# Attention scores over one head's 64 rows, the two heads alternating between the halves of TensorE

## The chip, the cores and the metric

The kernel runs on one core of a Trainium2 chip. The core's engines work side by side: TensorE (PE) multiplies matrices into PSUM, VectorE (DVE), ScalarE (ACT) and GpSimd (POOL) do the elementwise work, and SyncE (SP) issues most DMA. What counts is the device time of one execution in microseconds (us), as the median of several runs.

## The reference

What is computed is one attention block followed by two feed-forward blocks, over 4 batches, 8 heads, 576 tokens and 64 elements per head (512 per token):

```python
scores = (1 / sqrt(64)) * q @ k.T                 # per batch and head, 576 x 576
scores = where(pos[:, None] // 64 >= pos[None, :] // 64, scores, -1e9)
attn = softmax(scores) @ v                        # heads side by side give x, 576 x 512
x = x + relu(layernorm(x) * g @ w1_1) @ w2_1      # first feed-forward, 512 -> 2048 -> 512
u = x + real(fft(fft(x, tokens), features))       # mixing
out = u + relu(layernorm(u) @ w1_2) @ w2_2        # second feed-forward
```

## The kernel before, in words

Heads are taken two at a time: 4 batches of 4 pairs. The 64 elements of one head lie on partitions 0 to 63 and those of the other on 64 to 127, so q and k of a pair fill 128 partitions. A product of one head alone then has to keep the other head out, and the kernel does that with zeros: one operand is held with zeros in the other head's half, and the product runs over all 128 partitions.

The attention has two parts. The early queries (`e_...`, the first 256 tokens of each batch) are handled first, in f32: `e_raw` loads q of a pair and, into halves 1 and 2 of a tile `rz` whose other halves were set to zero once, k of the one and of the other head. There are three such tiles (`RAWE`), used in turn. `e_s` multiplies them into a score tile `st` of two PSUM banks, one per head, for a query block of 128 (128 keys) and a second one (256 keys), and `mask` adds a large negative number to the last 64 keys of the rows that may not see them (a product of the constant tiles `late` and `never`).

The late queries (`a_...`) come as f16 high and low parts. `a_split` writes q into `qz`, again with zeros in the other head's half, and k into `k`. `a_s` handles one of three query blocks j of a pair: for j = 2 (384 keys) and j = 3 (512 keys) three passes per head (high by high, low by high, high by low), all three of one head and then all three of the other, and two masks; for j = 4 (576 keys) 64 queries of each head share a product over all 128 partitions. `a_exp` takes the maximum on VectorE and the exponential on ScalarE, `a_norm_p` splits the result, a DMA transposes it, `a_pv` multiplies by the values.

All of it is recorded by one planner, `merge`, which takes the next step of several streams (early attention, late attention, feed-forward blocks, weight decoding) by due times made of fixed costs; a tile framework then orders single instructions by priority and by its own model of when each can start. Each engine executes its instructions in the order so fixed. Between two attention steps on TensorE stand one or two feed-forward blocks (`gemm1` at L626, `gemm2` at L651 and L678). The second half of the program (mixing and the second feed-forward) holds no attention.

Lines of before: `e_raw` loads at L882 and L885, `mask` at L917, `e_s` at L949, `a_s` at L1164, value products at L897, zeroing of `rz` at L1589.

Of the kernel before, what the change touches and what calls it, by code (L numbers as in the profile page):

```python
# [8 lines left out]
F32 = mybir.dt.float32  # L9
# [11 lines left out]
NPAIR = H // 2  # L21
# [8 lines left out]
RAWE = 3  # L30
# [68 lines left out]
def fused_kernel(ctx: ExitStack, tc: tile.TileContext, io: dict):  # L99
    nc = tc.nc  # L100
# [33 lines left out]
    late = cpool.tile([128, 3, 128], BF16, name="late")  # L134
    never = cpool.tile([128, 64], BF16, name="never")
# [668 lines left out]
    A = {}  # L804
    ap_ = {}

    def prio(f, n=None):
        def g(*a):
            if (n or AP) <= 0:
                return f(*a)  # L810
            with tc.high_priority(n or AP):
                return f(*a)
        return g
# [6 lines left out]
    def a_tile(shape, dt, tag, name):  # L820
        return ap_["p"].tile(shape, dt, tag=tag, bufs=ap_["b"][tag], name=name)
# [56 lines left out]

    def e_raw(b, p):

        r = A["rz"][(NPAIR * b + p) % RAWE]
        nc.sync.dma_start(out=r[:, 0], in_=io["qt"][b, p][:, S:S + 256])  # L882
        for h in range(2):
            hs = slice(64 * h, 64 * h + 64)
            nc.sync.dma_start(out=r[hs, 1 + h], in_=io["kt"][b, p][hs, 0:256])  # L885
        A["raw", b, p] = r

    def v_tiles(n, name):
# [23 lines left out]
        )  # L912
        A["ev", b] = (vh, vl, s)

    def mask(out, k):

        nc.tensor.matmul(out=out, lhsT=late[:, k, :], rhs=never, start=False, stop=True)  # L917

    def p_split(e, P, n):

# [22 lines left out]
    @(lambda f: prio(f, ESP))  # L943
    def e_s(b, p):
        r = A.pop(("raw", b, p))
        st = pss.tile([128, 2, 512], F32, tag="s", name="st")
        for t, (o, w) in enumerate(EO):
            for h in range(2):
                nc.tensor.matmul(  # L949
                    out=st[:, h, o:o + w], lhsT=r[:, 0, 128 * t:128 * t + 128], rhs=r[:, 1 + h, 0:w],  # L950
                    start=True, stop=False,
                )
            for h in range(2):
                mask(st[:, h, o + w - 64:o + w], 0)
        A["st", b, p] = st

    def e_exp(b, p):
# [85 lines left out]
    def e_items(b):  # L1043
        def head():
            e_raw(b, 0)
            e_load(b)

        def front(p):
            if p + 1 < NPAIR and b not in ET:
                e_raw(b, p + 1)  # L1050
            e_s(b, p)
            e_exp(b, p)
            e_norm_p(b, p)
# [5 lines left out]
        def two():  # L1059
            for p in range(2):  # L1060
                e_s(b, p)
                e_exp(b, p)
            in_order(lambda: (busy(NBUSY, A["busy"][:, 0:384]), e_norm_p(b, 0)) if b == 0 else e_norm_p(b, 0))

        if b in ET:
            return [
                (0.0, lambda: [e_raw(b, p) for p in range(3 if b == 0 else 2)], (), None),
                (4.0, lambda: (two(), e_load(b)), (), None),
                (2.0, lambda: (e_raw(b, 2) if b else None, e_norm_p(b, 1)), (), None),
                (3.0, lambda: (e_raw(b, 3), front(2), back(0)), (), None),  # L1070
                (3.0, lambda: (front(3), back(1)), (), None),
                (1.0, lambda: back(2), (), None),
                (1.0, lambda: back(3), (), ("X1", ("E", b))),
            ]
# [77 lines left out]
    @prio  # L1152
    def a_s(u, j):
        qz, k = A["op", u][0]
        st = pss.tile([128, 2, 512], F32, tag="s", name="st")
        sf = st.rearrange("p a f -> p (a f)")
        w = 128 * j + (128 if j < 4 else 64)
        for o in range(0, w, 512):
            n = min(w - o, 512)
            for h in range(2 if j < 4 else 1):  # L1160
                q = 384 * h + 128 * (j - 2)
                passes = ((0, 0), (1, 0), (0, 1))
                for i, (a, c) in enumerate(passes):
                    nc.tensor.matmul(  # L1164
                        out=st[:, h, 0:n] if j < 4 else sf[:, o:o + n],
                        lhsT=qz[:, a, q:q + 128], rhs=k[:, c, o:o + n],
                        start=(i == 0), stop=(j == 4 and i == 2),
                    )
        if j < 4:
            for h in range(2):  # L1170
                mask(st[:, h, w - 64:w], j - 1)
        A["st", u, j] = st[:, :, 0:w] if j < 4 else sf[:, 0:w].rearrange("p (o k) -> p o k", o=1)

    def a_exp(u, j):
# [85 lines left out]
    def attention_items(order):  # L1260
# [14 lines left out]
        for t, (u, j) in enumerate(units):  # L1275
            at(t, RK[0], a_s, u, j)
            at(t + lag[1], RK[1], a_exp, u, j)
            at(t + lag[2], RK[2], a_norm_p, u, j)
            at(t + lag[3], RK[3], a_pv, u, j)
            at(t + lag[4], RK[4], a_evac, u, j)  # L1280
            if j == 4 and u[1] == NPAIR - 1:
                at(t + lag[5], RK[5], a_x, u[0])
                gives[t + lag[5]] = ("X1", ("F", u[0]))
# [263 lines left out]
    if True:  # L1547
# [5 lines left out]
        nc.vector.memset(late, 0.0)  # L1553
        nc.vector.memset(never, float(-2.0 ** 120))
        for k, a, z in ((0, 0, 64), (1, 0, 32), (1, 33, 64), (1, 127, 128), (2, 64, 128)):
            nc.vector.memset(late[0:1, k, a:z], 1.0)
        F3 = ("F", 3)
        EF = [(h, b) for h in "EF" for b in range(B)]
        order1 = [x if x == "L" else (x[0], int(x[1])) for x in ORDER1.split()]
# [23 lines left out]
        A["busy"] = g_tile([128, 512], "busy")  # L1583
        busy(8, A["busy"][:, 0:384])
        A["unit"] = a_tile([128, 128], F32, "unit", "unit")
        A["rz"] = [a_tile([128, 3, 256], F32, "rz", f"rz{i}") for i in range(RAWE)]
        for z in A["rz"]:
            for h in range(2):
                nc.gpsimd.memset(z[64 - 64 * h:128 - 64 * h, 1 + h], 0.0)  # L1589
        nc.gpsimd.dma_start(out=A["unit"], in_=io["c_unit"])  # L1590
        w_signs(ap_["p"], WN[0], NZ[0])
        AE = [e_items(b) for b in range(B)]
# [209 lines left out]
```

## Time and profile before

| | us |
|---|---|
| median of 3 runs | 990.58 (988.44 to 992.95) |
| profiled execution | 996.84 |
| its span, first to last instruction | 995.0 |
| TensorE busy in the span | 937.5 (94%) |
| VectorE busy | 707.0 (71%) |
| ScalarE busy | 541.6 (54%) |
| mean granted clock of TensorE | 0.984 of full speed |

Busy time is what the records of an engine cover. A matmul's record reaches from its start to a modelled end, and the next one starts before that end; so from start to start is what a product costs in a row of products, and the record's own length is longer. Idle time of an engine that is not the bound costs nothing.

### The profile page before, as it was taken

How to read it: one execution, taken by the hardware profiler on the slowest of the kernel's cores; microseconds unless marked ns; L12 is line 12 of the kernel's file. 1: busy time of each engine (PE TensorE's matmuls, PEld its weight loads, DVE VectorE, ACT ScalarE, POOL GpSimd, SP SyncE). 2: the span in 40 equal slices, each digit the busy share in tenths (PEclk: the TensorE clock that was granted, in tenths of full speed). 3: DMA queues.
4: the chain of work that ended last, by engine and by line, in shares of the span. 5: the costliest groups of instructions: out<-in, count | busy, mean ns of one | idle time of the engine just before them, and what ended most of it. 6: DMA issues, size and time to landing. Idle time of an engine off the chain costs nothing.

```text
span 995.0 us, 19877 instructions
## 1 busy us (share of the span) xinstructions
PE 937.5 (94%) x7854; PEld 708.1 (71%) x7854; DVE 707.0 (71%) x1754; ACT 541.6 (54%) x964; POOL 78.4 (8%) x190
## 2 busy tenths in 40 slices
PE   8897899999898999998899799999999999999998
PEld 7795754665674764857485566858588888888887
DVE  3778898787777776556487878569476775765754
ACT  5778757777676776427466644325153352342431
POOL 2000010002011020040022111100000000000000
PEclk9898999999999999999999989999999999999999
DMA  8756546679567674587318666001110101101100
GB/s 254 226 180 204 151 98 141 139 130 180 108 149 142 130 141 90 97 192 276 106 47 237 216 189 212 16 12 64 43 23 23 33 22 33 22 23 43 22 23 22
DMA packets 159453, 110.97 MB, mean 112 GB/s; under 512 B 134397, under 2 KB 141574, under 8 KB 157312
## 3 DMA queue, kind: packets, MB, share of 16 engines
q1 hardware_dynamic: 154896, 104.87, 40.6%
q0 software_dynamic: 2352, 4.32, 1.9%
q8 instruction: 61, 1.00, 0.4%
q10 hardware_dynamic: 2112, 0.52, 0.2%
q14 instruction: 32, 0.26, 0.1%
HBM read 64.19 MB, written 11.01 MB: 76 GB/s over the span
## 4 chain that ended last, share of the span: by engine, by line
PE 42%; DVE 6%; DMA 5%; ACT 3%; issue 1%; POOL 0%; SPq 0%; ACTq 0%; POOLq 0%
PE g L697 15%; PE s L747 13%; PE g L626 5%; PE g L678 4%; PE g L651 3%; DMA wr<-in_w 3%; ACT junk L238 1%; DVE wq L338 1%; DVE ws L217 1%; DMA xnT1('F', 3)_7111<-xs 1%; DMA xnT2('F', 0)_8367<-xs 1%; ACT sign L216 1%; PE ya L1452 1%; DVE hT L636 1%; PE pq L1486 0%
## 5 line engine op out<-in xcount | busy, mean ns | idle before, releaser
L626 PEld LDWEIGHTS <-wq 128*128 128x128 f16 x2112 | 205.3, 99 | 43.9 <-issue 11.6
L651 PE MATMUL g<-wq,hT 128*128 128x512 f16 x768 | 182.4, 384 | 2.8 <-ACT hT L635 2.3
L697 PEld LDWEIGHTS <-wq 128*128 128x128 f16 x1344 | 131.5, 98 | 15.4
L651 PEld LDWEIGHTS <-hT 128*128 128x128 f16 x768 | 74.4, 99 | 89.6 <-issue 4.3
L747 PEld LDWEIGHTS <-hs 128*128 128x128 f16 x1176 | 115.1, 98 | 13.3
L714 ACT ACTIVATE hr<-g,tk 128x256 f32<-128x256 f32 x112 | 47.1, 472 | 141.0 <-PE g L697 141.0
L897 PE MATMUL pv<-vh,PT 128*128 128x65 f16 (+1 forms) x704 | 93.5, 200 | 12.7 <-DMA PT<-P 5.7
L722 DVE TENSOR_TENSOR hr<-hr 128x128 f32<-128x128 f32 x224 | 65.5, 292 | 48.3 <-ACT hr L714 40.3
L897 PEld LDWEIGHTS <-PT 128*128 128x128 f16 x1056 | 73.4, 98 | 20.6 <-issue 8.6
L1186 ACT ACTIVATE e<-st,aq,acf 128x384 f32<-128x384 f32 (+2 forms) x80 | 56.8, 742 | 48.2 <-DVE aq L1181 33.6
L922 DVE SCALAR_TENSOR_TENSOR P<-e,P 128x768 f16<-128x768 f32 (+2 forms) x56 | 54.6, 975 | 37.6 <-ACT P L921 37.5
L747 PE MATMUL s<-tT,hs 128*128 128x256 f16 x672 | 75.6, 273 | 0.0
L636 DVE SCALAR_TENSOR_TENSOR hT<-g,hT 128x512 f16<-128x512 f32 x88 | 59.8, 683 | 21.8 <-ACT hT L635 21.8
L635 ACT ACTIVATE hT<-g 128x512 f16<-128x512 f32 x88 | 51.4, 587 | 30.7 <-PE g L626 30.3
L678 PE MATMUL g<-wq,hT 128*128 128x512 f16 x288 | 64.4, 379 | 0.0
L1164 PE MATMUL st<-k,qz 128*128 128x512 f16 (+2 forms) x288 | 57.3, 330 | 6.9 <-ACT e L1186 6.3
L729 DVE TENSOR_TENSOR hs<-hr,hs 128x896 f16<-128x896 f32 x56 | 60.7, 1084 | 0.5
L216 ACT ACTIVATE sign<-wr 128x512 f16<-128x512 bf16 (+1 forms) x48 | 46.3, 968 | 23.0 <-DMA wr<-in_w 19.6
L897 PE MATMUL pv<-vl,PT 128*128 128x64 f16 (+1 forms) x352 | 58.0, 199 | 0.0
L747 PE MATMUL s<-tB,hs 128*128 128x256 f16 x504 | 57.3, 273 | 0.0
L217 DVE SCALAR_TENSOR_TENSOR ws<-wr,sign 128x512 int32<-128x512 int32 (+1 forms) x48 | 41.3, 865 | 19.7 <-ACT sign L216 17.9
L728 ACT ACTIVATE hs<-hr 128x896 f16<-128x896 f32 x56 | 53.1, 947 | 1.6 <-DVE hr L722 1.6
(434 smaller groups left out, 1607.7 us busy)
## 6 DMA issues: line engine op xcount, KB each, us to landing
wr<-in_w SPq DMA_DIRECT2D x16, 1023.5 KB, 5.6
wr<-in_w SPq DMA_DIRECT2D x32, 511.8 KB, 5.2
rawv<-in_vt SPq DMA_DIRECT2D x16, 320.0 KB, 3.5
rawqk<-in_kt SPq DMA_DIRECT2D x16, 288.0 KB, 2.9
d<-ws SPq DMA_DIRECT2D x4, 1024.0 KB, 5.1
ws<-d SPq DMA_DIRECT2D x4, 1024.0 KB, 5.8
wt<-d SPq DMA_DIRECT2D x4, 1024.0 KB, 4.8
rawqk<-in_qt SPq DMA_DIRECT2D x32, 80.0 KB, 2.9
```

The lines of the kernel that those rows point to most:

```text
L216: nc.scalar.activation(out=z[:, :, :, 1], in_=r.bitcast(BF16)[:, :, :, 2], func=AF.Copy)
L626: nc.tensor.matmul(out=ps[:, i, :], lhsT=w1(ffn, k, wh, m), rhs=xt[:, xh, k, :], start=(n == 0), stop=(n == 3 * KT - 1),)
L636: nc.vector.scalar_tensor_tensor(out=h[:, :, 1, :], in0=ps, scalar=0.0, in1=h[:, :, 0, :], op0=ALU.max, op1=ALU.subtract,)
L651: nc.tensor.matmul(out=ps, lhsT=h[f // 4][:, f % 4, hh, t * 128:(t + 1) * 128], rhs=w2(ffn, f, wh), start=(f == 0 and hh == 0 and wh == 0) ...
L678: nc.tensor.matmul(out=g2["b"][t], lhsT=h[f // 4][:, f % 4, hh, t * 128:(t + 1) * 128], rhs=w2(ffn, f, wh), start=(f == 0 and hh == 0 and ...
L697: nc.tensor.matmul(out=ps[:, q, :], lhsT=w1(2, k, wh, i + 8 * q), rhs=xt[:, xh, k, :], start=(n == 0), stop=(n == 3 * KT - 1),)
L722: done = nc.vector.tensor_tensor(out=r[:, o], in0=r[:, a], in1=r[:, b], op=op)
L729: nc.vector.tensor_tensor(out=h[:, 1], in0=r[:, 1:8], in1=h[:, 0], op=ALU.subtract)
L747: nc.tensor.matmul(out=ps, lhsT=h[:, hh, hb], rhs=T[nm][:, wh, i], start=(i == 0 and hh == 0 and wh == 0), stop=(i == 7 and hh == 1),)
L897: nc.tensor.matmul(out=out[..., 0:w], lhsT=l, rhs=v[..., 0:w], start=(n == 0), stop=(n == len(mm) - 1))
L1164: nc.tensor.matmul(out=st[:, h, 0:n] if j < 4 else sf[:, o:o + n], lhsT=qz[:, a, q:q + 128], rhs=k[:, c, o:o + n], start=(i == 0), stop=(j ...
L1186: nc.scalar.activation(out=e[:, h], in_=st[:, h], func=AF.Exp, scale=cf, bias=nb[:, h:h + 1],)
```

## The change

Three things change. `e_raw` loads all of k of a pair at once into a tile of two parts, a new one from the pool for each pair, and the zero halves and their memsets are gone. `e_s`, `a_s` for j = 2 and 3, and `mask` take their operands from 64 partitions, the lower for the first head and the upper for the second. And `a_s` has the loop over the passes outside that over the heads, so that the heads, and with them the halves of the array and the two banks, alternate from product to product. `late` gets its ones in row 64 too, so that the upper half's mask finds them.

```diff
 def e_raw(b, p):
-        r = A["rz"][(NPAIR * b + p) % RAWE]
+        r = a_tile([128, 2, 256], F32, "rz", f"rz{b}{p}")
         nc.sync.dma_start(out=r[:, 0], in_=io["qt"][b, p][:, S:S + 256])
-        for h in range(2):
-            hs = slice(64 * h, 64 * h + 64)
-            nc.sync.dma_start(out=r[hs, 1 + h], in_=io["kt"][b, p][hs, 0:256])
+        nc.sync.dma_start(out=r[:, 1], in_=io["kt"][b, p][:, 0:256])
...
-    def mask(out, k):
-
-        nc.tensor.matmul(out=out, lhsT=late[:, k, :], rhs=never, start=False, stop=True)
+    HALF = (slice(0, 64), slice(64, 128))
+
+    def mask(out, k, h):
+
+        nc.tensor.matmul(
+            out=out, lhsT=late[HALF[h], k, :], rhs=never[HALF[h]], start=False, stop=True
+        )
...
-                    out=st[:, h, o:o + w], lhsT=r[:, 0, 128 * t:128 * t + 128], rhs=r[:, 1 + h, 0:w],
-                    start=True, stop=False,
+                    out=st[:, h, o:o + w], lhsT=r[HALF[h], 0, 128 * t:128 * t + 128],
+                    rhs=r[HALF[h], 1, 0:w], start=True, stop=False,
                 )
             for h in range(2):
-                mask(st[:, h, o + w - 64:o + w], 0)
+                mask(st[:, h, o + w - 64:o + w], 0, h)
...
-            for h in range(2 if j < 4 else 1):
-                q = 384 * h + 128 * (j - 2)
-                passes = ((0, 0), (1, 0), (0, 1))
-                for i, (a, c) in enumerate(passes):
+            for i, (a, c) in enumerate(((0, 0), (1, 0), (0, 1))):
+                for h in range(2 if j < 4 else 1):
+                    q = 384 * h + 128 * (j - 2)
+                    r = HALF[h] if j < 4 else slice(0, 128)
                     nc.tensor.matmul(
                         out=st[:, h, 0:n] if j < 4 else sf[:, o:o + n],
-                        lhsT=qz[:, a, q:q + 128], rhs=k[:, c, o:o + n],
+                        lhsT=qz[r, a, q:q + 128], rhs=k[r, c, o:o + n],
...
-            nc.vector.memset(late[0:1, k, a:z], 1.0)
+            for r in (0, 64):
+                nc.vector.memset(late[r:r + 1, k, a:z], 1.0)
...
-        A["rz"] = [a_tile([128, 3, 256], F32, "rz", f"rz{i}") for i in range(RAWE)]
-        for z in A["rz"]:
-            for h in range(2):
-                nc.gpsimd.memset(z[64 - 64 * h:128 - 64 * h, 1 + h], 0.0)
```

First, where the loads stand at the program's start on SyncE's queue: `rz` are the tiles of early q and k, `wr` the first feed-forward's raw weights. Before:

```order
2 L882 DMA rz_113<-in_qt 128x256
3 L885 DMA rz_113<-in_kt 64x256 x2
4 L882 DMA rz_114<-in_qt 128x256
5 L885 DMA rz_114<-in_kt 64x256 x2
6 L882 DMA rz_115<-in_qt 128x256
7 L885 DMA rz_115<-in_kt 64x256 x2
8 L201 DMA wr_188<-in_w_1 128x2x2047
```

In this place two loads of k became one, and nothing else moved:

```order
2 L882 DMA rz_121<-in_qt 128x256
3 L883 DMA rz_121<-in_kt 128x256
4 L882 DMA rz_124<-in_qt 128x256
5 L883 DMA rz_124<-in_kt 128x256
6 L882 DMA rz_127<-in_qt 128x256
7 L883 DMA rz_127<-in_kt 128x256
8 L201 DMA wr_184<-in_w_1 128x2x2047
```

Second, TensorE in the early part, a pair of the last batch: `st<-rz` are its score products (L949, now L951), `st<-never,late` the masks, `g<-wq,hT` feed-forward. Before:

```order
1228 L949 MATMUL st<-rz_113 128x128
1229 L678 LDWEIGHTS hT
1230 L678 MATMUL g_1587<-wq_1550,hT 128x512
...
1239 L949 MATMUL st<-rz_113 128x128
1240 L678 LDWEIGHTS hT
1241 L678 MATMUL g_1587<-wq_1550,hT 128x512
1242 L917 LDWEIGHTS late
1243 L917 MATMUL st<-never,late 128x64
```

After the change, the same pair, and ahead of it one of the pairs that still alternate with feed-forward products (`g<-xnT1,wq`, L626), as 5 of the 16 pairs do, here and in before:

```order
812 L951 MATMUL st<-rz_1098 128x128
813 L626 LDWEIGHTS wq_459
814 L626 MATMUL g_1148<-xnT1('E', 1)_848,wq_459 128x256
815 L951 MATMUL st<-rz_1098 128x128
...
1234 L951 MATMUL st<-rz_1484 128x128 x2
1235 L917 LDWEIGHTS late
1236 L917 MATMUL st<-never,late 128x64
```

So single pairs close up, and others stay apart. In the late part the sequence of `a_s`, value and feed-forward blocks on TensorE is the same in both programs; each `a_s` call for j = 2 and 3 stands as one piece of six products and two masks.

## Rows read from the trace of the kernel before

**Rows 1.** The page's busy line, and TensorE's busy and clock slices.
```profile
PE 937.5 (94%) x7854; PEld 708.1 (71%) x7854; DVE 707.0 (71%) x1754; ACT 541.6 (54%) x964; POOL 78.4 (8%) x190
...
PE   8897899999898999998899799999999999999998
...
PEclk9898999999999999999999989999999999999999
```
**Rows 2.** Windows: busy us of each engine in four stages; columns stand first.
```profile
core 0: us, PE busy (x) PEld busy (x) DVE busy (x) ACT busy (x) POOL busy (x), PEclk, DMA share, GB/s
0.00:150.00 150.00, 131.31 (x1073) 104.70 (x1074) 112.32 (x301) 105.74 (x172) 13.91 (x37) 0.95 0.62 185
150.00:425.00 275.00, 255.96 (x2401) 172.03 (x2400) 208.68 (x527) 192.67 (x349) 27.41 (x73) 0.99 0.64 131
425.00:575.00 150.00, 136.32 (x921) 90.70 (x919) 104.94 (x284) 87.28 (x177) 28.31 (x58) 0.98 0.60 185
575.00:995.00 420.00, 413.89 (x3465) 340.70 (x3463) 281.10 (x646) 155.94 (x268) 8.75 (x24) 0.99 0.17 47
```
**Rows 3.** TensorE's waits, 150 to 425 us: us in total, times, longest.
```profile
PE st L1164 <- ACT e L1186: 6.3, 6, 1.5
PE g L626 <- DVE hT L636: 5.0, 7, 1.5
```
**Rows 4.** Timeline of TensorE: start us, us, what, at two late score calls.
```profile
285.99 1.46 PE L1164 MATMUL st<-k,qz 128*128 128x512 f16 x6
287.28 0.22 PE L917 MATMUL st<-never,late 128*128 128x64 bf16 x2
...
296.44 1.14 PE L1164 MATMUL st<-k,qz 128*128 128x384 f16 x6
297.41 0.22 PE L917 MATMUL st<-never,late 128*128 128x64 bf16 x2
297.47 1.89 PE L651 MATMUL g<-wq,hT 128*128 128x512 f16 x8
```
**Rows 5.** Groups by form: late products of 512 columns, busy us and mean ns.
```profile
L1164 PE MATMUL st<-k,qz 128*128 128x512 f16 x144 | 36.3, 379 | 6.4 <-ACT e L1186 6.3
```
**Rows 6.** Timeline of TensorE where early scores (f32) alternate with feed-forward products.
```profile
101.07 0.27 PE L626 MATMUL g<-xnT1('E', 1)_852,wq 128*128 128x256 f16 x1
101.18 0.60 PE L949 MATMUL st<-rz 128*128 128x256 f32 x2
101.62 0.27 PE L626 MATMUL g<-xnT1('E', 1)_852,wq 128*128 128x256 f16 x1
101.73 0.60 PE L949 MATMUL st<-rz 128*128 128x256 f32 x2
```
**Rows 7.** Groups by form: products over 128 and over 98 rows, mean ns.
```profile
L1452 PE MATMUL ya<-c_ct,ge 128*128 128x289 f16 x72 | 10.7, 287 | 0.0
...
L1452 PE MATMUL ya<-c_ctl,gS 98*128 98x289 f16 x12 | 3.4, 287 | 0.0
```
**Rows 8.** Weight loads of L1164 (ns min/median/max), and small value products on the timeline.
```profile
L1164 PEld LDWEIGHTS <-qz x288: 95/98/99, 152.4 to 407.8; 128*128 128x128 f16 x144
...
258.36 0.22 PE L897 MATMUL pv<-vh,PT 128*128 128x65 f16 x2
258.42 0.19 PE L897 MATMUL pv<-vl,PT 128*128 128x64 f16 x1
258.45 0.22 PE L897 MATMUL pv<-vh,PT 128*128 128x65 f16 x2
```
**Rows 9.** Timeline of the start, all engines.
```profile
0.73 2.11 POOL L1589 MEMSET rz<- 64x256 f32 x6 [0.29 <-POOLq L1772]
...
1.67 1.20 SPq L885 DMA_DIRECT2D rz<-in_kt  x2
...
4.84 0.77 PE L949 MATMUL st<-rz 128*128 128x128 f32 x2 [0.87 <-DMA rz<-in_kt]
```
**Rows 10.** Windows: a stretch of the early stage.
```profile
70.00:80.00 10.00, 5.99 (x49) 4.95 (x47) 9.41 (x27) 8.58 (x11) 1.22 (x3) 1.00 0.52 169
```

More of the change, by code (lines that the diff above doesn't have):

```diff
@@ L1170, in a_s @@
             for h in range(2):
-                mask(st[:, h, w - 64:w], j - 1)
+                mask(st[:, h, w - 64:w], j - 1, h)
         A["st", u, j] = st[:, :, 0:w] if j < 4 else sf[:, 0:w].rearrange("p (o k) -> p o k", o=1)
```

## The prediction

> **What bounds the kernel now.** I read first the page's busy shares and slices. [rows 1] show TensorE busy for 94% of the span, and hardly a slice below eight tenths. That is a mean over stages, so next come the busy times of four stages [rows 2]. From 575 us to the end TensorE is busy 413.89 of 420 us: that part gets shorter only by less TensorE work, and this change has no instruction in it; it only starts it sooner or later. From 150 to 425 us, where the late queries' attention runs, TensorE is busy 255.96 of 275 us (93%), VectorE 208.68 (76%), ScalarE 192.67. So TensorE is the nearest bound there, VectorE the next. From 0 to 150 us (early queries and weight decoding) no engine is full: TensorE 131.31, VectorE 112.32, DMA share 0.62. Then I asked what TensorE waits for between 150 and 425 us: the longest total is 6.3 us, scores' products waiting for a bank that ScalarE still reads [rows 3]. There is no large stall that a shorter product would run into at once, because feed-forward products stand between the attention steps. Last, two stretches of the timeline give the price of the products [rows 4].
>
> **Part 1: late scores, a_s for j = 2 and j = 3.** [rows 4] show both calls. For j = 3 six products of 512 columns start at 285.99 us and the masks at 287.28: 1.29 us, 215 ns each. For j = 2 six products of 384 columns start at 296.44, the masks at 297.41: 0.97 us, 162 ns each. There are 16 pairs of heads, so these products take 16 x 2.26 = 36.2 us of TensorE's time. After the change each product uses 64 rows of the array, the two heads alternate, and each writes its own bank. If the two halves run side by side, half goes: 18.1 us. If they don't, nothing goes: a product over 98 rows lasts the 287 ns of one over 128 [rows 7], so fewer rows alone buy nothing. No row shows two products side by side; the ends are 0 and 18.1 us. I take 18.1, because a full-height product already takes one column a cycle in these rows (512 columns in 215 ns at the granted 2.4 GHz), and the other half of the array was multiplying zeros in that time; nothing has to move faster than now.
>
> The Trainium skill has a measured packing for this ("TensorE: Matmul & The Clock Gate", Part 3): four tiles of 32 rows ran 3.07 times as fast as one after the other. Estimated from that page at the same efficiency, two tiles would run 1.53 times as fast, and the 18.1 us would be 12.6. No row here shows it.
>
> The masks, two per call, start 0.03 us apart [rows 4]. Side by side one of two goes: 32 x 0.03 = 1.0 us. Parts together: 19 us.
>
> **Part 2: the change between whole and half array.** In the changed order TensorE passes 178 times between the two forms: 64 times around the 32 calls of a_s, which stay in one piece (twelve rows and the masks, then feed-forward or value products), and 114 times in the early stage, where e_s is mixed with feed-forward products (second part of the order shown above). No row of before has such a change. The lower bound is zero: TensorE passes from f16 feed-forward products to f32 scores and back with the same 0.11 us from start to start as within feed-forward, and two f32 passes of 256 columns take their 0.44 us and no more [rows 6]. The upper bound is a full emptying: a 512-column product lasts 379 ns by its record [rows 5] and the next starts after 215, so 164 ns of tail, and then a weight load of 98 ns [rows 8] that nothing covers: 262 ns. I take 60 ns: the next product's weight load loses its cover, which costs between 30 ns (products of 64 and 65 columns, each with its own load, start that far apart [rows 8]) and 98 ns. In a_s that is 64 x 0.06 = 3.8 us, in the early stage 114 x 0.06 = 6.8 us.
>
> **Part 3: early scores, e_s.** In f32 a product is two passes, both of the lower half and then both of the upper, so at best the second pass of one lies beside the first of the other: one pass saved in four, 0.11 us at 128 columns and 0.22 at 256 [rows 6]. In the new order 9 of 32 narrow and 10 of 32 wide pairs are adjacent; the rest have a feed-forward product between them. That is 9 x 0.11 + 10 x 0.22 = 3.2 us less.
>
> **Part 4: the start and the loads.** Six memsets (2.11 us on GpSimd) go, and 16 loads of k become one instead of two; a pair of them holds SyncE's queue for 1.20 us [rows 9]. The first scores wait for the second load of k, which lands at 4.84 us. Between 0 and 2 us could be gained; one load's issue is 0.6 us, and I take 1 us. The bytes are the same, the later loads are prefetched behind weight loads, and five more one-row memsets on VectorE lie beside DMA issue, so nothing more is counted.
>
> **How much of it reaches the end.** In the late stage 15.2 us (19 less 3.8) leave TensorE's work. If TensorE were the bound all the time, all would arrive; if VectorE took over, little. At 70 to 80 us VectorE is 9.41 of 10 us busy and TensorE falls to 5.99 [rows 10]: this is what a stretch looks like where VectorE decides. The late stage has VectorE at 76%; squeezed by 15 us it would be at 80%. I take three quarters (bounds one half and one): 11.4 us. The order of attention steps and feed-forward blocks on TensorE is the same in both programs, so everything behind moves up with it. In the early stage TensorE has idle time of 19 of 150 us, partly waits for data, so I count half of 6.8 - 3.2 = 3.6 us: 1.8 us longer. Sum: -11.4 + 1.8 - 1 = -10.6 us. With c as the price of a change in us, the sum is -16.9 + 105 c.
>
> The sum is made against the profiled execution, 996.84 us (span 995.0), which gives 986.2. That execution lies 6.3 us above the median of the runs, 990.58, so against the median it is **980.0 us**.
>
> **Rival A: the array is emptied at each change** (slower). The price is 0.164 to 0.262 us at 178 places. The sum is zero at c = 0.161 and passes +5 us at 0.21; with 0.262 it is +10.6 us, 1001 us. For it: the early stage changes form at nearly every e_s product, between single feed-forward products. Against: the f32/f16 alternation costs nothing [rows 6], and the 32 late calls change only twice each. At 0.164 the result is 991 us, no change.
> The Trainium skill states this as a rule ("TensorEngine Tiling (Array Packing)", Tiling Modes, Key Properties): changing the tiling mode, not just the tile, drains TensorE. It gives no duration, and no row here shows one.
>
> **Rival B: the halves run one after the other**, so the change doesn't do what it says. Then parts 1 and 3 give nothing, and the changes cost 105 x 0.06 = 6.3 us, less 1 us at the start: 990 us with free changes, 996 us with these. For it: no row shows two products at once. Against: the two write different banks and read different partitions.
>
> **Rival C: the chain from maximum over exponential to split** (VectorE and ScalarE) sets the late stage. Then TensorE waits longer where it now waits 6.3 us [rows 3], and 2 to 5 us are left: 986 to 990 us. For it: VectorE is 76% busy and a_s already waits for banks. Against: 93% on TensorE.
>
> **How the numbers follow.** A difference of 0.5% (5 us) is about what a measurement of this kernel can tell from no change. Forecast (side by side, a change under 0.11 us): 0.55, all of it faster, 967 to 985 us. Rival A: 0.22, of which 0.12 is slower by over 5 us and 0.10 within. Rival B: 0.13, 0.07 slower and 0.06 within. Rival C: 0.10, within. Together: faster 0.55, same 0.26, slower 0.19. With free changes and three quarters arriving the time is 973.7 us, with all arriving and both other gains some 967; the dear end of A is 1001. The range 969 to 998 leaves out the last few of either.
>
> **What the profile after would show.** Side by side: six 512-column products of a_s take 0.65 us in place of 1.29, starts in pairs a few ns apart. Price of a change: the gap from the last feed-forward product before a_s to the first of a_s beyond its 0.11 or 0.215 us, and the same behind the masks. Share: the late stage 11 us shorter with TensorE's busy share still over 90%; if VectorE's rises while TensorE's falls and the stage stays at 275 us, rival C. Early stage: 150 us a little longer. The forecast is wrong if the pairs' starts are 215 ns apart, or if gaps of over 0.16 us stand at the changes.

## The result, and the profile after

The changed kernel takes **997.44 us** (median of 9 runs, 994.65 to 1002.62) against 990.58 (9 runs): ratio 1.0078, interval 1.0055 to 1.0101. It is slower by about 7 us, where 980.0 was forecast; the range 969 to 998 holds the time, the sign is wrong. The profiled execution of after took 996.99 us (span 995.2), close to its median, while that of before lay 6 us above its own. The two spans, 995.2 and 995.0, are therefore no comparison; the medians are. One execution of late_new below (997.61 us, granted clock 0.942, against 978.84 to 985.10 in its other five) is left out of its median and its ratio.

The page of after, TensorE's busy line and slices as in [rows 1]:

```profile
PE 934.1 (94%) x7854; PEld 693.6 (70%) x7854; DVE 704.5 (71%) x1759; ACT 542.4 (54%) x964; POOL 75.6 (8%) x184
...
PE   8898999988888898998999899999999999999998
```

The same two stages of after as in [rows 2] (columns as there):

```profile
0.00:150.00 150.00, 136.70 (x1054) 100.42 (x1055) 108.61 (x294) 105.59 (x168) 11.14 (x30) 0.94 0.63 183
150.00:425.00 275.00, 243.76 (x2357) 157.38 (x2356) 206.09 (x526) 192.92 (x351) 27.64 (x73) 0.99 0.66 132
```

In the late stage TensorE is busy 12.2 us less than before (243.76, was 255.96), though its window also holds 44 products fewer. In the early stage it is busy 5.4 us more with 19 products fewer done. The early loss stayed and the late saving vanished. First the saving itself: timeline of TensorE, after, at two late score calls (start us, us, what), to be laid beside [rows 4]:

```profile
286.31 0.66 PE L1166 MATMUL st<-k,qz 64*128 64x384 f16 x6
286.81 0.19 PE L917 MATMUL st<-never,late 64*128 64x64 bf16 x2
286.94 1.05 PE L626 MATMUL g<-xnT1('E', 3)_3148,wq 128*128 128x256 f16 x8
...
289.94 0.27 PE L626 MATMUL g<-xnT1('E', 3)_3148,wq 128*128 128x256 f16 x1
290.14 0.82 PE L1166 MATMUL st<-k,qz 64*128 64x512 f16 x6
290.80 0.19 PE L917 MATMUL st<-never,late 64*128 64x64 bf16 x2
290.93 0.20 PE L895 MATMUL pv<-vl,PT 128*128 128x64 f16 x1
```

From the first product to the masks, six products of 384 columns take 0.50 us (0.97 before), six of 512 take 0.66 (1.29). The halves do run side by side. The price of a change of form stands beside it: from the last feed-forward product to the first score product 0.20 us (289.94 to 290.14), where 0.11 is usual after 256 columns; from the masks to the next whole product 0.13, where it was 0.06.

The waits of TensorE from 150 to 425 us, after, as in [rows 3]:

```profile
PE st L1166 <- ACT e L1188: 11.0, 7, 2.4
PE g L626 <- DVE hT L636: 7.8, 9, 1.5
```

They were 6.3 and 5.0: the first two places to look for the lost saving. The late stage, from the first to the last product of `a_s`, after (ns min/median/max, first and last start):

```profile
L1166 PE MATMUL st<-k,qz x288: 192/354/387, 156.8 to 412.1; 64*128 64x384 f16 x48, 64*128 64x512 f16 x48, 128*128 128x512 f16 x32, 128*128 128x64 f16 x16
```

That is 255.3 us; before it was 152.4 to 407.8, 255.4 us [rows 8]. The stage is as long as it was, though TensorE has some 12 us less to do in it, and it starts 4.4 us later.

### The profile page after: what moved, and what is told of

It is laid out like the page before. It is cut to its first block, busy times and chain, and to the rows that moved or that the text cites. A ratio compares the mean times of both kernels' runs of the same rounds, so it can differ in the third digit from the quotient of the medians.

```text
span 995.2 us, 19849 instructions
## 1 busy us (share of the span) xinstructions
PE 934.1 (94%) x7854; PEld 693.6 (70%) x7854; DVE 704.5 (71%) x1759; ACT 542.4 (54%) x964; POOL 75.6 (8%) x184
## 4 chain that ended last, share of the span: by engine, by line
PE 42%; DVE 7%; DMA 5%; ACT 3%; issue 1%; POOL 0%; ACTq 0%; POOLq 0%; DVEq 0%; SPq 0%
PE g L697 15%; PE s L747 13%; PE g L626 5%; PE g L678 4%; PE g L651 3%; DMA wr<-in_w 2%; DMA xnT1L<-xs 1%; ACT junk L238 1%; DVE wq L338 1%; DVE ws L217 1%; DMA xnT2('F', 0)_8363<-xs 1%; DVE hT L636 1%; ACT sign L216 1%; PE ya L1454 1%; PE pq L1488 1%
## 5 line engine op out<-in xcount | busy, mean ns | idle before, releaser
L626 PEld LDWEIGHTS <-wq 128*128 128x128 f16 x2112 | 206.0, 99 | 48.4 <-issue 20.3
L651 PEld LDWEIGHTS <-hT 128*128 128x128 f16 x768 | 74.0, 98 | 87.7 <-issue 3.3
L678 PEld LDWEIGHTS <-hT 128*128 128x128 f16 x288 | 28.4, 99 | 33.7 <-issue 2.6
```

The lines of the kernel that those rows point to most:

```text
L626: nc.tensor.matmul(out=ps[:, i, :], lhsT=w1(ffn, k, wh, m), rhs=xt[:, xh, k, :], start=(n == 0), stop=(n == 3 * KT - 1),)
L651: nc.tensor.matmul(out=ps, lhsT=h[f // 4][:, f % 4, hh, t * 128:(t + 1) * 128], rhs=w2(ffn, f, wh), start=(f == 0 and hh == 0 and wh == 0) ...
L678: nc.tensor.matmul(out=g2["b"][t], lhsT=h[f // 4][:, f % 4, hh, t * 128:(t + 1) * 128], rhs=w2(ffn, f, wh), start=(f == 0 and hh == 0 and ...
```

## The experiments

Each run was timed beside the kernel before; its median there was 990.76 to 991.62 us. Ratios below are to that, with their interval. **One part alone, and a probe of TensorE's worth.**

*late_only*: the late half of the change; the early part is that of before.

```diff
-            for h in range(2 if j < 4 else 1):
-                ...
-                        lhsT=qz[:, a, q:q + 128], rhs=k[:, c, o:o + n],
+            for i, (a, c) in enumerate(((0, 0), (1, 0), (0, 1))):
+                for h in range(2 if j < 4 else 1):
+                    ...
+                        lhsT=qz[r, a, q:q + 128], rhs=k[r, c, o:o + n],
```

> Half-height products in the late part alone (a_s for j = 2 and 3); the early part with its three-part tiles, zero halves and full-height products as before. By the trace after the change this takes some 12 us of TensorE's work out of the late stage, the price of 64 changes of form already taken off. Theory 1 (the loss comes from 114 changes in the early part; the late gain is lost because VectorE and ScalarE set the late stage): within 3 us of before. Rival (the late gain does arrive by three quarters, and the early part loses twice as much as it seems): about 9 us faster. Second rival (the late part is where the loss is made): 5 to 8 us slower.

Measured: 992.74 us, 1.0021 (0.9998 to 1.0043). The late part alone gains nothing.

*early_only*: the early half of the change; `a_s` is that of before.

```diff
-                    out=st[:, h, o:o + w], lhsT=r[:, 0, 128 * t:128 * t + 128], rhs=r[:, 1 + h, 0:w],
+                    out=st[:, h, o:o + w], lhsT=r[HALF[h], 0, 128 * t:128 * t + 128],
+                    rhs=r[HALF[h], 1, 0:w], start=True, stop=False,
```

> Half-height products, the two-part tile and the single load of k in the early part alone; the late part as before. Theory 1: 5 to 8 us slower than before, as the whole change. First rival: some 16 us slower. Second rival: within 3 us of before.

Measured: 996.85 us, 1.0053 (1.0031 to 1.0075). This is most of the loss: 5.3 and 2.1 thousandths against the change's 7.8.

*two_pass*: before, full height, with less TensorE work in the late stage.

```diff
-                passes = ((0, 0), (1, 0), (0, 1))
+                passes = ((0, 0), (1, 0), (0, 1)) if j == 4 else ((0, 0), (1, 0))
```

> The kernel before with the third of the three passes left out of a_s for j = 2 and 3 (queries high by keys low), all at full height: 12 us of TensorE's work less in the late stage, as much as the half-height products save there, and no change of form at all. Theory 1: within 3 us of before, since TensorE does not set that stage. Rival (three quarters of a saving arrive): 9 us faster.

Measured: 979.73 us, 0.9902 (0.9867 to 0.9938). Read alone, this says that TensorE's time does arrive, and that late_only is a puzzle. But the framework that issues the kernel plans the order of all engines by its own model. In the trace of late_only VectorE's and ScalarE's order is that of before; in two_pass the framework planned these two engines anew. So two_pass changed two things, and the runs with the order held fixed, further down, separate them.

*early_block*: early_only with the priority of early scores raised, so that a call's products stand together: 26 changes of form in place of 114.

```diff
-    @(lambda f: prio(f, ESP))
+    @(lambda f: prio(f, 2000))
     def e_s(b, p):
```

> As early_only, but the early score products have so high a priority that feed-forward products no longer come between them: 26 changes of form in place of 114, and 29 of 32 pairs adjacent. If the changes make the early loss (theory 1): within 3 us of before. If the loads, the pool's tiles or the shuffled order on the other engines make it: still 5 us slower.

Measured: 982.55 us, 0.9914 (0.9883 to 0.9946). Within 3 us of before was expected at best; the same half-height products that cost 5 us when scattered are in a kernel that gains 8 us.

**The order held fixed, late part.** In these runs the order of VectorE and ScalarE is imposed by edges that set the issue order and add no wait; TensorE's order of blocks in the late stage is the same in all. SyncE's queue is not imposed: in before_new 10 of its 289 loads and transposes stand elsewhere than in before, so that run does not part the two engines' order from theirs.

```diff
+        for name, seq in ORDER.items():
+            mine = [i for i in nc.cur_bb.bb.instructions if i.engine == getattr(mybir.EngineType, name) and i.opcode not in QUIET]
+            for x, y in zip(seq, seq[1:]):
+                tc.add_manual_dep(mine[y], mine[x].name, mybir.DependencyInfo(NoSync, DATA))
```

*before_new* is the kernel before with this loop and nothing else, `ORDER` being VectorE's and ScalarE's order in two_pass.

> The kernel before with VectorE's and ScalarE's instructions in the order of two_pass and nothing else changed. Theory O: within 4 us of before, since TensorE's work is what that order frees. Rival L (the order alone is the gain, and TensorE's saving has no part in it): some 10 us faster.

Measured: 983.17 us, 0.9919 (0.9895 to 0.9942). The order alone, with every product of before, gives 8 of two_pass's 11 us.

*late_new* is late_only's edit with the same loop and table.

> late_only with VectorE's and ScalarE's instructions in the order that the tile framework chose for two_pass, where it saw the shorter products; TensorE's order is the same in both. Theory O (the half-height products do save some 11 us of TensorE's work, but the order of the other two engines was planned for products of full price, and waits eat the saving): 7 to 10 us faster than before. Rival P (the half-height products' own costs eat it, whatever the order): 1 to 3 us slower than before, as late_only.

Measured: 982.78 us, 0.9917 (0.9888 to 0.9945): the same as before_new. The time lies where theory O put it, but not by the half height, which again adds nothing.

*two_pass_old* is two_pass's edit with the loop and the order of before.

> two_pass (the third pass of a_s left out for j = 2 and 3, full height, no change of form) with VectorE's and ScalarE's instructions held to the order that they have in the kernel before. Theory O: the saving of 12 us is mostly lost, within 4 us of before. Rival P: as two_pass, some 10 us faster.

Measured: 985.33 us, 0.9946 (0.9926 to 0.9966). At the order of before, a third fewer products give 5 us, between the two expectations; half-height products, saving about as much, give none. That difference is not settled (below).

The stage in late_only, before_new and late_new (first and last start of `a_s` products):

```profile
L1167 PE MATMUL st<-k,qz x288: 192/354/634, 153.0 to 408.3; 64*128 64x384 f16 x48, 64*128 64x512 f16 x48, 128*128 128x512 f16 x32, 128*128 128x64 f16 x16
...
L1219 PE MATMUL st<-k,qz x288: 193/356/624, 149.6 to 395.3; 128*128 128x512 f16 x80, 128*128 128x384 f16 x48, 128*128 128x64 f16 x16
...
L1253 PE MATMUL st<-k,qz x288: 192/354/387, 150.4 to 395.4; 64*128 64x384 f16 x48, 64*128 64x512 f16 x48, 128*128 128x512 f16 x32, 128*128 128x64 f16 x16
```

255.3, 245.7 and 245.0 us: the stage follows the plan of the other engines, not the height of the products. How it does so is seen where TensorE waits for a bank. Timeline of TensorE, before (in brackets the idle time ahead and what ended it):

```profile
176.54 0.81 PE L1164 MATMUL st<-k,qz 128*128 128x512 f16 x3 [1.15 <-ACT e L1186]
...
224.08 0.81 PE L1164 MATMUL st<-k,qz 128*128 128x512 f16 x3 [1.32 <-ACT e L1186]
```

The same two places in late_only:

```profile
177.27 0.81 PE L1167 MATMUL st<-k,qz 128*128 128x512 f16 x3 [1.63 <-DVE aq L1184]
...
224.87 1.16 PE L1167 MATMUL st<-k,qz 128*128 128x512 f16 x3 [2.12 <-ACT e L1189]
```

Counted from each kernel's first `a_s` product (152.4 and 153.0), TensorE is released after 24.1 and 71.7 us in before, after 24.3 and 71.9 in late_only. It arrives earlier, waits longer (1.15 and 1.32 become 1.63 and 2.12 us) and goes on at the same time. So it is all along the stage: counted in this way, the 48 calls of `a_s` start in late_only between 0.6 us before and 1.9 us after their time in before.

**VectorE's work cut.** *before_pmax_old* is before, its own order imposed, with the maximum in `a_exp` over the first 128 keys alone.

```diff
-        nc.vector.tensor_reduce(out=mx, in_=st, axis=AX.X, op=ALU.max)
+        nc.vector.tensor_reduce(out=mx, in_=st[:, :, 0:128], axis=AX.X, op=ALU.max)
```

> The kernel before in its own order, with a_exp's maximum taken over the first 128 keys of a row alone: some 25 us of VectorE's work less in the late stage, TensorE's the same. Theory C (the chain over VectorE and ScalarE sets the late stage): 8 us faster or more. Rival (TensorE sets it): within 3 us of before.

Measured: 978.17 us, 0.9872 (0.9845 to 0.9899).

*late_pmax_old* is late_only with that line, its own order (that of before) imposed.

> late_only with the same short maximum, in late_only's order (that of before). Theory C: with VectorE out of the way the half-height products' 11 us on TensorE show, and it is 4 us or more faster than before_pmax_old. Rival P (the half-height products' own costs eat their gain): the same as before_pmax_old or slower.

Measured: 979.85 us, 0.9891 (0.9864 to 0.9919). Less VectorE work is worth 12.7 us without any change on TensorE (the profiled stage shows 9 of them: 246.5 us, was 255.4). The half height adds nothing even then, against theory C's expectation and as rival P had it; whether rival P's reason holds is seen below, where the saving is traced. Busy times in the same 245 us of before and of before_pmax_old (columns as in [rows 2]):

```profile
150.00:395.00 245.00, 226.72 (x2074) 148.15 (x2073) 190.50 (x480) 179.63 (x328) 24.90 (x67) 0.99 0.66 136
...
150.00:395.00 245.00, 232.86 (x2156) 153.62 (x2155) 169.23 (x490) 184.96 (x337) 25.04 (x68) 1.00 0.70 140
```

VectorE falls from 190.50 to 169.23 us and TensorE gets 82 more products done in the window, at 95% busy in place of 93%.

*new_pmax* is before_new with that line, *late_new_pmax* is late_new with it.

> before_new (two_pass's order on VectorE and ScalarE, full height, all passes) with a_exp's maximum over the first 128 keys alone. If VectorE still sets the late stage in that order: 5 us or more faster than before_new. If something else does (TensorE, ScalarE or the transposes): within 3 us of before_new.

> late_new (half-height late products, two_pass's order) with the same short maximum. If TensorE is what is left as the bound of new_pmax: 5 us or more faster than new_pmax. If not: the same within 3 us.

Measured: 970.42 us, 0.9785 (0.9761 to 0.9808), and 969.40 us, 0.978 (0.9752 to 0.9808). The short maximum is worth 13 us in the better order too. The profiled stage of late_new_pmax is 3.5 us shorter than that of new_pmax (234.8 and 238.3), but the times do not differ.

**The early part, order held fixed.** *early_old* is early_only with the loop and the order of before on TensorE, VectorE and ScalarE: 122 changes of form. *before_early* is before, full height, with the order of early_only on the three engines.

> early_only (half-height early products, two-part tile, one load of k) with TensorE's, VectorE's and ScalarE's instructions held to the order of the kernel before: 122 changes of form. Theory S (the changes' price on TensorE, some 0.1 us each, makes the early loss): 4 to 7 us slower than before. Theory Q (the shuffled order of the engines makes it): within 2 us of before.

> The kernel before, full height, zero halves and its own loads, with TensorE's, VectorE's and ScalarE's instructions in the order of early_only: no change of form. Theory S: within 2 us of before. Theory Q: 4 to 7 us slower.

Measured: early_old 998.68 us, 1.008 (1.0051 to 1.0108); before_early 987.96 us, 0.9969 (0.9951 to 0.9987). So the early half of the change, its products scattered, costs 8 us in either order (1.008 against 1; 1.0053 against 0.9969), and the order that the framework planned for early_only is by itself 3 us better than that of before. First and last start of `a_s`, early_old:

```profile
L1266 PE MATMUL st<-k,qz x288: 192/356/379, 160.8 to 416.2; 128*128 128x512 f16 x80, 128*128 128x384 f16 x48, 128*128 128x64 f16 x16
```

The late stage starts 8.4 us later than in [rows 8] and lasts the same 255.4 us: all of the early cost arrives.

*before_block* is before, full height, with early_block's priority.

> The kernel before with the high priority of early_block for the early score products, at full height: no change of form. If closing up the early products is what made early_block 8 us faster: about 8 us faster than before here too. If half-height products in pairs make it (some 5 us of TensorE's work) and the priority only spares the changes: within 3 us of before.

Measured: 987.17 us, 0.9952 (0.9931 to 0.9972), between the two expectations. The priority alone gives about 4 us; early_block, with half height in closed blocks, has about 4 us more (0.9914). That these are the half height's is not shown: the intervals overlap, and VectorE's and ScalarE's order, not imposed here, differs between the two programs. Timeline of TensorE, a full-height call of before_block:

```profile
92.86 0.71 PE L949 MATMUL st<-rz 128*128 128x128 f32 x4
93.41 0.22 PE L917 MATMUL st<-never,late 128*128 128x64 bf16 x2
93.47 1.11 PE L949 MATMUL st<-rz 128*128 128x256 f32 x4
94.41 0.22 PE L917 MATMUL st<-never,late 128*128 128x64 bf16 x2
```

And a call of early_block:

```profile
73.52 0.49 PE L950 MATMUL st<-rz 64*128 64x128 f32 x4 [0.80 <-ACT e L968]
73.84 0.20 PE L918 MATMUL st<-never,late 64*128 64x64 bf16 x2
73.87 0.68 PE L950 MATMUL st<-rz 64*128 64x256 f32 x4
74.38 0.20 PE L918 MATMUL st<-never,late 64*128 64x64 bf16 x2
```

From first product to masks a pair takes 0.32 us in place of 0.55 at 128 columns and 0.51 in place of 0.94 at 256. Closed, the f32 pairs too nearly halve: in early_block's records the four passes of a pair start as two couples (73.515 and 73.521, 73.728 and 73.735 us). What happens to scattered ones is seen in after, in the stretch of batch 1's feed-forward:

```profile
107.97 0.28 PE L626 MATMUL g<-xnT1('E', 1)_848,wq 128*128 128x256 f16 x1
108.18 0.20 PE L917 MATMUL st<-never,late 64*128 64x64 bf16 x1
108.31 0.28 PE L626 MATMUL g<-xnT1('E', 1)_848,wq 128*128 128x256 f16 x1
...
108.66 0.28 PE L626 MATMUL g<-xnT1('E', 1)_848,wq 128*128 128x256 f16 x1
108.87 0.70 PE L951 MATMUL st<-rz 64*128 64x256 f32 x2
109.50 0.28 PE L626 MATMUL g<-xnT1('E', 1)_848,wq 128*128 128x256 f16 x1
```

Each feed-forward product now holds TensorE for 0.21 us in place of 0.11, a mask for 0.13 in place of 0.03, a lone score product for 0.63 in place of 0.44 [rows 6]. Of the last 0.19 us only 0.09 are the change back. The other 0.10 lie inside the product: its second pass starts 0.32 us after its first (0.22 in before), and the first of its two weight loads starts with the product, where in before it started 0.11 us ahead (TensorE's load queue, at the same place):

```profile
108.87 0.29 PEld L951 LDWEIGHTS st<-rz 64*128 64x128 f32 x2
```

**Both findings put together.** *best_full* is early_block with VectorE's and ScalarE's late order from a plan made as for two_pass, all products of `a_s` there and of full height; *best_half* has half height in the late part too.

> early_block's early part (half-height products in closed blocks) with VectorE's and ScalarE's late order taken from the program that was planned with two passes; late products at full height, all three passes. If the two gains are independent: about 16 us faster than before. If they overlap: 8 to 10 us.

> best_full with half-height products in the late part too. If other engines set the late stage in this order as well (theory C): within 3 us of best_full. Rival (in the better order TensorE sets it): 5 to 8 us faster than best_full.

Measured: 971.68 us, 0.9804 (0.9779 to 0.9828), and 972.25 us, 0.9799 (0.9774 to 0.9823). Both compute all that the reference asks and beat both kernels by 18 us or more; the late half height is again worth nothing. The page of best_full (span 967.6 us):

```profile
PE 922.8 (95%) x7854; PEld 697.8 (72%) x7854; DVE 702.1 (73%) x1759; ACT 538.7 (56%) x964; POOL 77.3 (8%) x184
```

**Where the late saving went.** Five pairs of kernels differ by the late half of the change alone. From the first to the last product of `a_s`, before and late_only (columns as in [rows 2]):

```profile
152.40:407.80 255.40, 237.12 (x2193) 156.48 (x2192) 196.15 (x488) 183.82 (x334) 24.94 (x67) 0.99 0.65 134
153.00:408.30 255.30, 229.16 (x2192) 146.64 (x2193) 195.52 (x485) 183.67 (x333) 24.99 (x67) 0.98 0.67 133
```

The same for all five pairs, full height / half height, in us of the profiled executions:

| pair | stage | TensorE busy | TensorE idle |
|---|---|---|---|
| before / late_only | 255.4 / 255.3 | 237.1 / 229.2 | 18.3 / 26.1 |
| before_new / late_new | 245.7 / 245.0 | 235.9 / 226.2 | 9.8 / 18.8 |
| before_pmax_old / late_pmax_old | 246.5 / 245.3 | 234.5 / 225.0 | 12.0 / 20.3 |
| new_pmax / late_new_pmax | 238.3 / 234.8 | 232.8 / 222.4 | 5.5 / 12.4 |
| best_full / best_half | 245.8 / 244.6 | 233.9 / 223.7 | 11.9 / 20.9 |

So rival P's reason does not hold: the work does leave TensorE, 8 to 10 us net of the changes of form, and comes back as 7 to 9 us of waiting, nearly all of it for VectorE and ScalarE. A smaller part may go into the granted clock. Its mean over the executions is lower with half height in every pair, by 0.002 to 0.0035 (0.985 against 0.988 in late_only and before). As a share of the whole time that is about 2 to 3 us, an estimate and an upper one, since some of it falls where TensorE waits anyway.

## Why the prediction was wrong

**Part 1, right.** By the two calls shown, 16 x (0.47 + 0.63) = 17.6 us leave the late products, 18.1 were forecast. The 1.53 times estimated from the Trainium skill ("TensorE: Matmul & The Clock Gate", Part 3) was too low: 1.29 / 0.66 is 1.95.

**Part 2, the price mis-sized.** A change of form costs 92 to 107 ns (starts of consecutive records beyond the usual spacing), in f16, bf16 and f32 and in both directions, where 60 was taken; it lies inside the bounds 0 to 262. The upper end of the 30 to 98 ns for a weight load without cover would have been right. Rival A's cost at each change is there, but under the 0.161 us at which the forecast's sum turns. The Trainium skill ("TensorEngine Tiling (Array Packing)", Tiling Modes, Key Properties) says that changing the tiling mode drains TensorE; the runs show the 0.1 us, and not whether this is a drain. With 0.1 us in that sum the forecast would still have been faster, by 6.4 us. The sign did not fall here.

**Part 3, undersized.** It took the passes of a pair to run in program order, one of four side by side with another; the records show them start two by two, so half goes. Adjacent f32 pairs save 0.23 and 0.43 us, not 0.11 and 0.22, so the 9 and 10 adjacent pairs save some 6.4 us and not 3.2. (They are 9 of 16 and 10 of 16; the prediction's 32 is the count of products.) The net cost of the early part was still larger than forecast: 114 x 0.1 - 6.4 = 5 us by this count, 8 us in the two comparisons at a fixed order. The sum had no term for the 0.10 us inside a lone f32 product: the trace of early_only has 10 narrow and 11 wide of them, some 2 us more. That makes 7 of the 8, but the count is an estimate; for early_old, with more changes and fewer adjacent pairs, it gives more than the 8 us measured. The granted clock is lower as well (mean of 12 executions 0.985 in early_only, 0.990 in before_early), by estimate up to 5 us; how much of the 8 us that is was not tried.

**Part 4, not there.** The first scores start at 5.22 us in after, 4.84 in before [rows 9]; in the six profiles with a single load they start between 5.22 and 5.88, in the twelve with two between 4.79 and 5.17. The single load gained nothing here.

**How much reaches the end: here the sign fell.** Three quarters of the late saving and one half of the early cost were to arrive; it was none and all. 93% busy [rows 2] was read as "TensorE sets the late stage". But TensorE met the other engines at the same places at the same times, with half height or without (late_only). The stage shortened by 9 to 10 us when the order of VectorE and ScalarE was changed (before_new), or when VectorE's maximum was shortened (before_pmax_old), and in five settings half height moved the time by at most 2 us. With the measured shares the sum is 0 for the late part and +8 for the early part in the order of before; the new order gives back 3, and the late part's 2 us (not distinguishable from none) make about 7. That is the measured difference; as these shares are differences between the runs themselves, it says that the parts add up and no more.

**Rival C** named the mechanism (the chain over maximum, exponential and split), at 0.10 and with 2 to 5 us left; what was left was nothing, and the early cost decided the sign. What it lacked is that order counts: the sum priced instructions and left out that a plan of the other engines is worth 3 us early and 8 us late. **Rival B** fell.

**Open.** Why two_pass_old gains 5 us at the order of before where late_only gains none. There 10 us less of work become 4 us of waiting, and the stage is 6 us shorter (249.3 us); so work taken from TensorE is not always lost. Two waits for a bank, 1.02 and 1.53 us in before, are 0.26 and 0.14 us there, and nothing shows why. Late_only's profile also has the stage at half clock for 3 short stretches where before has one and two_pass_old two: by estimate 3 us against before, 2 against two_pass_old, but no run separated it. And whether it is VectorE's total work or the length of the chain through its maximum that sets the stage: the short maximum cuts both.

## What to carry to other kernels

A busy share of 93% does not say that an engine sets the pace: look whether it is released by others at places spread over the stage, and test by cutting the other engine's work or fixing its order. Half-height products on separate row groups halve a paired stretch, but each switch between half and whole height costs about 0.1 us: here they lost 8 us when scattered among whole products, and lost nothing in closed blocks. When a scheduler plans the order, an edit also changes the plan; hold the order fixed before crediting the edit.

## What the runs showed of the hardware

Two f16 products over 64 rows each, in different halves and to different banks, start 3 to 4 ns apart and together last as long as one of full height: 0.22 us for 512 columns. In f32 the couples start 6 to 7 ns apart, and a pair of 256 columns takes 0.51 us in place of 0.94. That the f32 pair gains nearly as much as the f16 pair was not expected. Nor was the weight load at a change of form. On TensorE's load queue in after (start us, us, what), around the call at 290.14 us:

```profile
289.91 0.10 PEld L626 LDWEIGHTS <-wq 128*128 128x128 f16 x1
290.14 0.33 PEld L1166 LDWEIGHTS <-qz 64*128 64x128 f16 x6
```

The load for the first half-height product starts at 290.14, with the product itself and 0.20 us after the start of the whole product ahead of it (289.94, 256 columns, 0.11 us of spacing). Between whole products the load runs ahead, beside the previous product (289.91, ahead of 289.94); at this change it starts only when that product's columns have passed and some 0.09 us more are gone.
